# The background work of an eighteen-unit Strassen stage is placed step by step, and part of it changes engine

## The chip, the cores and the metric

The kernel runs on one core of one Trainium2 chip. The metric is the device time of one execution in microseconds (us). A program on this core issues instructions in a fixed order on each of five engines: TensorE (PE, matmuls; its weight loads are listed apart as PEld), VectorE (DVE), ScalarE (ACT), GpSimd (POOL) and SyncE (SP, which issues the DMAs). An engine that waits for something holds up all that stands behind it in its own order.

## The reference

```
attn = softmax-with-decay attention of q, k, v, f          (4 batches, 8 heads, 576 rows, 64 columns)
x    = attn, heads side by side                            (2304 x 512)
x    = (sigmoid(x @ w_gate) * (x @ w_val)) @ w_out         (w_gate, w_val: 512 x 1536, w_out: 1536 x 512)
logits = x @ router                                        (2304 x 8)
each token goes to one of 8 experts, at most 288 tokens each, in the order of the logits
out  = relu(x[mask_e] @ w1[e]) @ w2[e]                     (per expert, 512 -> 1024 -> 512)
```

## The kernel before

The program has five stretches: attention up to 195 us, the gated product with w_gate and w_val by a Strassen scheme (195 to 608 us), the product with w_out together with the router's dots (608 to 757 us), the routing, and the experts up to the end.

Because the order decides the experts, products are made in three passes: every operand is split into a high part (a copy by ACT into the matmul type) and a low part (the rest, a subtraction), and a product is high*high + high*low + low*high.

**The Strassen stage.** Class `Ffn`, method `unit` (L610). There are 18 units, listed in `UNITS`; a unit (p, t) makes columns p of gate and val for a third t of the tokens. It runs 14 products (`STEPS`: seven for gate, seven for val), each of six matmuls at L597. Units with t = 0 or 1 multiply 512 token columns at a time and are called wide here; those with t = 2 have 128 and are called narrow. Counted from 0 the narrow units are 3, 5, 8, 11, 14 and 15. Within a unit the base work is: ACT copies sums out of the accumulators (L620, L631) and takes the sigmoid (L641), DVE adds (L629), subtracts (L639) and multiplies gate by val (L647), SP stores (L605). PE waits for some of these: a product adds into an accumulator that an L629, L631 or L620 must have read or written.

**Background work.** While units run, operands of later ones are prepared. Class `Sets`: 48 pieces of weights come as 64-bit numbers and are packed to 32 bits by three DVE operations each (`bits`, L443, L445, L447). Pieces 0 to 23 go two by two into a set: tile `mb` holds the pair, four sums and differences of halves (`sums`, L465, L467, L468, L470, on DVE) make the Strassen operands, and ACT and GpSimd split them (`high` L484, `low` L488). There are 12 sets; a unit uses two. Pieces 24 to 47 are packed in the only buffer of tile `mw`, written back to memory by SP (`wf<-mw`, L450), and read again as w_out. Class `XOps` does the same for x: DVE multiplies the loaded attention result by the loaded 1/sum (`mult` L530, `mult_rest` L546), DVE adds (`add`, L551), and ACT and GpSimd or DVE split (L560, L564). Class `Out` splits w_out in 12 blocks (`weights`, L682, eight by GpSimd and four by DVE), and loads and splits the gated result (`load` L697, `split` L703, L704).

What sets their order: every unit gets one list of background operations, and after each product a like share of what is left of the list is issued:

```
n = -(-len(tasks) // (len(STEPS) - step))
for do in tasks[:n]:
    do()
tasks = tasks[n:]
```

The lists are filled in `network`: set 3 in unit 0, x of the second third in unit 1, x of the last third and the first pieces in unit 2, then a set or two with two pieces in each wide unit. The narrow units have no list. Pieces 32 to 37 stand in unit 13, 38 to 43 in unit 16, and 44 to 47 in unit 17, behind the splits of w_out; in unit 17 the first four splits of the gated result come last.

**After the stage.** `stream` (L722) makes one 128-token tile of x after another: 36 matmuls (L709), a copy by ACT into `mr`, a store, and eight dots on DVE with the router's columns (`dots`, L719). 12 of the 18 token tiles go this way, which makes 96 dots. The logits of the other six come from matmuls with a product of w_out and the router: `rest_logits` (L749 to L757) clears an accumulator on DVE at L753 and runs its matmuls, `logits` copies it (L765), transposes it on PE (L771) and copies it (L773). The matmuls at L757 therefore stand behind the DVE operations issued before L753.

Of the kernel before, what the change touches and what calls it, by code (L numbers as in the profile page):

```python
# [405 lines left out]
SEQ = list(range(12)) + sum(([12 + 2 * i, 13 + 2 * i, 24 + 2 * i, 25 + 2 * i] for i in range(4)), []) + list(range(20, 24)) + list(range(32, 48))  # L406
SLOT = {5: 0, 2: 1, 1: 2, 7: 3, 6: 4, 3: 5, 4: 6}
PART = {(0, 0): 2, (0, 1): 4, (1, 0): 3, (1, 1): 5}


class Sets:
# [19 lines left out]
    def bits(self, n, step, after=True):  # L431
        nc = self.ev.nc
        w = self.raw[n].bitcast(U32).rearrange("p (n t) -> p t n", t=2)
        if n < 2 * NF:
            if step == 0 and n % 2 == 0:
                self.b[n // 2] = self.mix.tile([128, 2, 512], U32, name="mb", bufs=1)
            b = self.b[n // 2][:, n % 2]
        else:
            if step == 0:
                self.b[n] = self.fw.tile([128, 512], U32, name="mw", bufs=1)  # L440
            b = self.b[n]
# [15 lines left out]
    def sums(self, s, step, tmp=None):  # L457
        nc = self.ev.nc
        b = self.halves(s)
        if step == 0:  # L460
# [4 lines left out]
            nc.vector.tensor_tensor(t, b[:, :, 0], b[:, :, 1], op=OP.add)  # L465
        elif step == 1:
            nc.vector.tensor_tensor(b[:, 1, 0], b[:, 1, 0], b[:, 0, 0], op=OP.subtract)  # L467
            nc.vector.tensor_tensor(b[:, 0, 1], b[:, 0, 1], b[:, 1, 1], op=OP.subtract)  # L468
        else:
            nc.vector.tensor_tensor(b[:, 0, 0], b[:, 0, 0], b[:, 1, 1], op=OP.add)  # L470
# [19 lines left out]
    def jobs(self, s):  # L490
        do = lambda f, *a: (lambda: f(*a))
        return [do(self.sums, s, 0), do(self.high, s, 2), do(self.sums, s, 1), do(self.low, s, 2), do(self.high, s, 0),
                do(self.low, s, 0), do(self.sums, s, 2), do(self.high, s, 1), do(self.low, s, 1)]

    def piece(self, n, after=True):
        do = lambda k: (lambda: self.bits(n, k, after))
        return [do(k) for k in range(3)]


class XOps:  # L500
# [1135 lines left out]
```

## Time and profile before

| what | us |
|---|---|
| runs shown: median (lowest, highest) of 3 | 1064.77 (1062.83, 1065.18) |
| the profiled execution | 1065.7 |
| its span, first to last instruction | 1063.5 |
| PE busy in the span | 953.4 (90%) |
| DVE, ACT, POOL busy | 597.8, 432.3, 475.6 |
| mean granted clock of TensorE, of full speed | 0.905 |

The span is what the trace shows, from the first instruction to the last; the profiled execution's time is 2.2 us longer. Stretches are given in us from the span's start. A row of the views below with an arrow names what an engine waited for and what ended the wait.

### The profile page before, as it was taken

The page shows a single profiled execution, that of the slowest core. Times are in us where ns is not written, and L with a number is a line of the kernel's source. Part 1 is how long each engine was busy: PE and PEld are TensorE (multiplying, and loading weights), DVE is VectorE, ACT ScalarE, POOL GpSimd, SP SyncE. Part 2 cuts the span into 40 slices and gives each one's busy share as a digit, 9 for nine tenths or more (in the row PEclk, how much of TensorE's full clock was granted, in tenths as well). Part 3 has the DMA queues.
Part 4 walks back from the last instruction along what each step waited for, and adds up shares of the span by engine and source line. Part 5 has one row for each costly group of instructions (what it writes and reads, how often), then busy time and mean ns, then how long its engine had stood idle before and what let it go on. Part 6 is the DMA issues. An engine that isn't in the chain of part 4 may idle for free. (4 is left out here: it accounts for less than half of the span.)

```text
span 1063.5 us, 15366 instructions
## 1 busy us (share of the span) xinstructions
PE 953.4 (90%) x5440; PEld 818.6 (77%) x5440; DVE 597.8 (56%) x1220; ACT 432.3 (41%) x798; POOL 475.6 (45%) x379
## 2 busy tenths in 40 slices
PE   8999999975799979897898679996599999999996
PEld 5787777753688778686796458885478999999996
DVE  6476755985544655657425649999554244333441
ACT  6777766642332333324212423222011554554431
POOL 7779886531111111112000438744022887777751
PEclk9999999997876978969659889899699999999998
DMA  4978786432322542534505767563112776666620
GB/s 125 256 213 209 206 229 166 132 91 72 109 59 59 149 131 71 151 112 139 161 18 168 267 238 278 178 229 116 48 41 81 224 225 205 199 198 182 197 91 29
DMA packets 92965, 160.87 MB, mean 151 GB/s; under 512 B 14995, under 2 KB 43059, under 8 KB 92758
## 3 DMA queue, kind: packets, MB, share of 16 engines
q1 hardware_dynamic: 88726, 148.34, 46.2%
q0 software_dynamic: 3072, 9.44, 2.7%
q10 hardware_dynamic: 1088, 2.10, 0.7%
q8 instruction: 43, 0.70, 0.3%
q14 instruction: 36, 0.29, 0.1%
HBM read 115.44 MB, written 35.01 MB: 141 GB/s over the span
## 5 line engine op out<-in xcount | busy, mean ns | idle before, releaser
L1095 POOL TENSOR_TENSOR elo<-eraw,ehi 128x1024 fp32r<-128x1024 f32 x46 | 110.9, 2421 | 34.8 <-ACT ehi L1093 34.5
L719 DVE CUSTOM_DVE_ANT_0 mb<-mr,bc 128x512 f32<-128x512 f32 x96 | 115.5, 1203 | 15.7 <-ACT mr L733 11.4
L160 PE MATMUL pv<-e,vf 128*65 128x256 f32 (+1 forms) x434 | 96.7, 360 | 0.0
L1189 PE MATMUL ey<-hh,ehi 128*128 128x288 f32 x256 | 77.8, 304 | 0.0
L1189 PE MATMUL ey<-hl,ehi 128*128 128x288 f32 x256 | 75.8, 296 | 0.5
L1189 PE MATMUL ey<-hh,elo 128*128 128x288 f32 x256 | 75.3, 294 | 0.0
L182 DVE CUSTOM_DVE_ANT_0 mj<-p1b,mq 128x192 bf16<-128x192 f32 (+1 forms) x116 | 42.3, 421 | 55.5 <-PE p1b L160 55.5
L160 PEld LDWEIGHTS pv<-e,vf 128*65 128x65 f32 x434 | 51.3, 139 | 21.2 <-issue 5.7
L1174 PE MATMUL eh<-xeh,ehi 128*128 128x288 f32 x224 | 67.6, 302 | 0.0
L1093 ACT ACTIVATE ehi<-eraw 128x1024 fp32r<-128x1024 f32 x60 | 63.4, 1056 | 9.3 <-DMA eraw<-w 9.3
L1174 PE MATMUL eh<-xeh,elo 128*128 128x288 f32 x224 | 65.9, 294 | 0.0
L1174 PE MATMUL eh<-xel,ehi 128*128 128x288 f32 x224 | 65.8, 294 | 0.0
L1177 DVE SCALAR_TENSOR_TENSOR hl<-eh,hh 128x288 fp32r<-128x288 f32 x64 | 29.1, 457 | 62.2 <-ACT hh L1176 52.0
L160 PE MATMUL p1b<-P 67*128 67x448 f32 (+2 forms) x244 | 58.6, 306 | 0.0
L682 POOL TENSOR_TENSOR wol<-wol,woh 128x512 fp32r<-128x512 f32 x8 | 12.0, 1526 | 98.7 <-ACT woh L682 98.7
L157 POOL TENSOR_TENSOR p<-raw,p 64x576 fp32r<-64x576 f32 x32 | 47.9, 1497 | 6.3 <-DMA p<-P 3.4
L647 DVE TENSOR_TENSOR q<-q,u 128x512 f32<-128x512 f32 (+1 forms) x36 | 25.8, 717 | 43.5 <-ACT u L620 43.5
L1176 ACT ACTIVATE hh<-eh 128x288 fp32r<-128x288 f32 x64 | 26.2, 411 | 57.2 <-PE eh L1174 41.8
L1189 PEld LDWEIGHTS ey<-hl,ehi 128*128 128x128 f32 x256 | 48.2, 188 | 1.6 <-DVE hl L1177 1.6
L704 POOL TENSOR_TENSOR a0l<-a0l,a0h 128x768 fp32r<-128x768 f32 x14 | 28.7, 2053 | 44.0 <-ACT a0h L703 41.9
L153 POOL TENSOR_TENSOR p<-raw,P 64x576 fp32r<-64x576 f32 x32 | 46.5, 1454 | 3.5 <-DMA p<-P 0.9
L1189 PEld LDWEIGHTS ey<-hh,ehi 128*128 128x128 f32 x256 | 48.1, 188 | 0.0
(603 smaller groups left out, 3013.3 us busy)
## 6 DMA issues: line engine op xcount, KB each, us to landing
eraw<-w SPq DMA_DIRECT2D x56, 512.0 KB
mr<-ww SPq DMA_DIRECT2D x36, 512.0 KB
gd<-q SPq DMA_DIRECT2D x96, 128.0 KB
p<-P SPq DMA_DIRECT2D x62, 144.0 KB
raw<-qk SPq DMA_DIRECT2D x15, 576.0 KB
wf<-mw SPq DMA_DIRECT2D x24, 256.0 KB
mr<-wt SPq DMA_DIRECT2D x12, 512.0 KB
a0l<-gd SPq DMA_DIRECT2D x14, 384.0 KB
```

Source lines behind the costliest of these rows:

```text
L153: nc.gpsimd.tensor_tensor(P2[h][64:128, :S], RAW[h][0:64], P1[h % 5][0:64, Q0:K0], op=OP.subtract)
L157: nc.gpsimd.tensor_tensor(p2[0:64, S:], r[64:128], p2[64:128, S:], op=OP.subtract)
L160: nc.tensor.matmul(out, lhsT, rhs, start=start, stop=stop, skip_group_check=True)
L182: nc.vector.tensor_tensor_reduce(out=junk[:, JT[t]:JT[t] + n], in0=src, in1=ev.mq[:, S - n:], op0=OP.add, op1=OP.min, scale=-1.0, scalar=3 ...
L704: (eng or nc.gpsimd).tensor_tensor(l, l.bitcast(F32), h, op=OP.subtract)
L719: nc.vector.tensor_tensor_reduce(out=junk, in0=x, in1=self.bc[:, e], op0=OP.mult, op1=OP.add, scale=1.0, scalar=0.0, accum_out=self.L[:, e ...
L1093: nc.scalar.activation(hi, r, AF.Copy)
L1095: eng.tensor_tensor(lo, r, hi, op=OP.subtract)
L1174: nc.tensor.matmul(p[:, :CH], w_[:, ws], x_[:, k], start=n == 0, stop=n == 11)
L1176: nc.scalar.activation(h[0][:, f], p[:, :CH], AF.Relu)
L1177: nc.vector.scalar_tensor_tensor(h[1][:, f], p[:, :CH], 0.0, h[0][:, f], op0=OP.max, op1=OP.subtract)
L1189: nc.tensor.matmul(p[:, :CH], w_[:, ws], h_[:, f], start=n == 0, stop=n == 23)
```

## The change

What it does:

1. Each background operation of the stage gets a step of its own, counted from 0 to 251 over the 18 units of 14 products, by `on(step, operation)`; `piece`, `wset` and `conv` place a piece, a weight set and an x operand. `unit` issues what stands at a step after its product. Narrow units have one piece each now, its three operations some four steps apart.
2. The four sums of weight halves go to GpSimd for sets 3 to 11. All low parts of x in the stage go to GpSimd (nine of them were on DVE), and so do all 12 splits of w_out.
3. Set 3 moves from unit 0 to steps 10 to 16. The x work of the second third is spread over units 0 to 2; x for the last third and its 1/sum are loaded ahead of the multiplications, in three groups, and multiplied in two operations instead of four.
4. The pieces above 30 use three buffers in turn (`mw` and the halves of `mb`). They stand two or three steps apart: 31 to 35 in units 12 and 13, one in each of units 14 and 15, 38 to 42 in unit 16, and 43 to 47 in unit 17, the last at step 247.
5. w_out is loaded at steps 224 to 235 (unit 16) and split at 227 to 238; the first four parts of the gated result are loaded at 238 and 239 and split at 242 to 246.
6. The accumulator of the router logits is cleared after 80 of the 96 dots instead of after all (`cleared`), in another bank.
7. In the attention, some loads of x are issued ahead of those of 1/sum.

The diff, cut to its core:

```
     def sums(self, s, step, tmp=None, eng=None):
+        eng = eng or self.ev.nc.gpsimd
...
-            nc.vector.tensor_tensor(t, b[:, :, 0], b[:, :, 1], op=OP.add)
+            eng.tensor_tensor(t, b[:, :, 0], b[:, :, 1], op=OP.add)
...
+                i = (n + 2) % 3 if n > 30 else 0
+                if i == 1:
+                    self.spare = self.mix.tile([128, 2, 512], U32, name="mb", bufs=1)
+                self.b[n] = self.spare[:, i - 1] if i else self.fw.tile([128, 512], U32, name="mw", bufs=1)
...
-    def mult_rest(self, k):
-        r = self.r4[:, k]
-        self.ev.nc.vector.tensor_tensor(r, self.x4[:, k], r, op=OP.mult)
+    def mult_rest(self, n):
+        x = self.x4[:, 2 * n:2 * n + 2]
+        self.ev.nc.vector.tensor_tensor(x, x, self.r4[n], op=OP.mult)
...
-    def unit(self, p, t, tasks):
+    def unit(self, n, plan):
...
-            n = -(-len(tasks) // (len(STEPS) - step))
-            for do in tasks[:n]:
+            for do in plan.pop(0, ()):
                 do()
-            tasks = tasks[n:]
+            for g in sorted(plan):
+                plan[g - 1] = plan.pop(g)
...
-        return [do(nc.scalar.activation, h, l.bitcast(F32), AF.Copy),
-                do((nc.vector if f % 3 == 2 else nc.gpsimd).tensor_tensor, l, l.bitcast(F32), h, op=OP.subtract)]
+        nc.scalar.activation(h, l.bitcast(F32), AF.Copy)
+        nc.gpsimd.tensor_tensor(l, l.bitcast(F32), h, op=OP.subtract)
...
+    def cleared(self):
+        self.lg = self.bank("o2")
+        self.ev.nc.vector.memset(self.lg[:, :256], 0.0)
...
     def rest_logits(self, raws):
-        self.lg = self.bank("o0")
-        nc.vector.memset(self.lg[:, :256], 0.0)
...
+        def on(g, f, *a, **k):
+            todo.setdefault(g, []).append(do(f, *a, **k))
...
+        def piece(n, *at):
+            for i, g in enumerate(at if len(at) == 3 else (at[0], at[0], at[-1])):
+                on(g, W.bits, n, i)
+
+        def wset(s, *at):
+            for n, g in enumerate(at if len(at) == 6 else [at[0] + i for i in (0, 1, 2, 3, 5, 6)]):
+                on(g, W.step, s, n)
...
+        wset(3, 10, 11, 12, 13, 15, 16)
...
+        on(24, lambda: X.load_x4(tmp["mr1"]))
+        on(22, lambda: X.load_r4(0, tmp["mb"][:, 512:]))
...
+        piece(8, 45, 49, 53)
+        piece(9, 56, 57)
+        wset(4, 58)
+        piece(24, 61, 62)
...
+        wset(11, 178)
+        for n, g in enumerate(((182, 183), (185, 186), (187, 188), (189, 190), (191, 192), (198, 202, 206), (212, 216, 220),
+                     (224, 225), (226, 227), (228, 229), (230, 231), (232, 233), (238, 239), (240, 241), (242, 243), (244, 245), (246, 247))):
+            piece(31 + n, *g)
...
+        for n in range(NF):
+            on(224 + n, O.load_weights, n)
+            on(227 + n, O.weights, n)
...
+        for n in range(4):
+            on(238 + n // 2, first, *divmod(n, 2))
+            on(242 + n + n // 2, O.split, line[n // 2], n % 2)
...
+        after[10][1].append(O.cleared)
```

How the order on the engines moves, at three places (`L` numbers are those of each program's own text; 128x512 is partitions by elements; `mr` is a piece as loaded, `q` and `u` are tiles of the unit's base work).

DVE in unit 13, the pieces; before:

```order
L447 SCALAR_TENSOR_TENSOR mw<-mr_4395,mw 128x512
L443 TENSOR_SCALAR mw<-mr_4410 128x512
L647 TENSOR_TENSOR q_4418<-q_4418,u_4449 128x512
L445 SCALAR_TENSOR_TENSOR mw<-mr_4410,mw 128x512
L447 SCALAR_TENSOR_TENSOR mw<-mr_4410,mw 128x512
L443 TENSOR_SCALAR mw<-mr_4432 128x512
L639 TENSOR_TENSOR q_4484<-gW,u_4474 128x512
L445 SCALAR_TENSOR_TENSOR mw<-mr_4432,mw 128x512
L647 TENSOR_TENSOR q_4461<-q_4461,u_4496 128x512
L447 SCALAR_TENSOR_TENSOR mw<-mr_4432,mw 128x512
L639 TENSOR_TENSOR q_4511<-gX,u_4487 128x512
L443 TENSOR_SCALAR mw<-mr_4465 128x512
```

and now:

```order
L445 TENSOR_SCALAR mb<-mr_4309 128x512
L447 SCALAR_TENSOR_TENSOR mb<-mr_4309,mb 128x512
L645 TENSOR_TENSOR vW<-u_4393,vD 128x512
L449 SCALAR_TENSOR_TENSOR mb<-mr_4309,mb 128x512
L445 TENSOR_SCALAR mb<-mr_4385 128x512
L447 SCALAR_TENSOR_TENSOR mb<-mr_4385,mb 128x512
L667 TENSOR_TENSOR q_4402<-q_4402,u_4433 128x512
L449 SCALAR_TENSOR_TENSOR mb<-mr_4385,mb 128x512
L445 TENSOR_SCALAR mw<-mr_4416 128x512
L447 SCALAR_TENSOR_TENSOR mw<-mr_4416,mw 128x512
L449 SCALAR_TENSOR_TENSOR mw<-mr_4416,mw 128x512
L659 TENSOR_TENSOR q_4472<-gW,u_4460 128x512
```

Before, the next piece's first operation (L443) writes the one buffer `mw` that the last piece's store still reads; now three pieces in a row have three different buffers (two of them halves of `mb`).

GpSimd in the middle of the stage, two weight sets before:

```order
L488 TENSOR_TENSOR a0l<-mb,a0h 128x512
L488 TENSOR_TENSOR a0l<-mw,a0h 128x512
L488 TENSOR_TENSOR a0l<-mb,a0h 128x768
L488 TENSOR_TENSOR a1l<-mb,a1h 128x512
L488 TENSOR_TENSOR a1l<-mw,a1h 128x512
L488 TENSOR_TENSOR a1l<-mb,a1h 128x768
```

and one set now:

```order
L467 TENSOR_TENSOR mw<-mb 128x512
L490 TENSOR_TENSOR a0l<-mb,a0h 128x512
L490 TENSOR_TENSOR a0l<-mw,a0h 128x512
L469 TENSOR_TENSOR mb<-mb 128x256
L470 TENSOR_TENSOR mb<-mb 128x256
L472 TENSOR_TENSOR mb<-mb 128x256
L490 TENSOR_TENSOR a0l<-mb,a0h 128x768
```

The four sums (L467, L469, L470 and L472) stand between the low parts (L490) now, where they were on DVE before.

DVE at the end of the router's dots; before:

```order
L719 ISA mb_6035,L_94<-mr1_6020,bc_5179 128x512
L719 ISA L_94 128x1
L719 ISA mb_6037,L_94<-mr1_6020,bc_5179 128x512
L719 ISA L_94 128x1
L753 MEMSET o0_6039 128x256
L1575 MEMSET mr0_6125 128x512
```

and now:

```order
L738 ISA mb_5899,L_94<-mr1_5884,bc_5167 128x512
L738 ISA L_94 128x1
L738 ISA mb_5901,L_94<-mr1_5884,bc_5167 128x512
L738 ISA L_94 128x1
L770 MEMSET o2_5946 128x256
L738 ISA mb_5951,L_94<-mr0_5948,bc_5167 128x512
L738 ISA L_94 128x1
```

The clearing of the accumulator (128x256) came behind the last dot; now it comes between the dots of the tenth tile and those of the eleventh.

## Rows read from the trace of the kernel before

**Rows 1.** Busy time by stretch. Columns: stretch, length, busy us by engine, granted clock, DMA share, GB/s.

```profile
195.50:215.00 19.50, 19.35 (x85) 15.69 (x84) 17.58 (x22) 11.57 (x20) 8.75 (x6) 1.00 0.66 187
215.00:241.00 26.00, 19.98 (x83) 14.85 (x82) 21.17 (x28) 10.72 (x20) 9.78 (x7) 1.00 0.28 83
215.00:280.10 65.10, 46.12 (x169) 34.33 (x168) 40.13 (x61) 25.56 (x50) 17.85 (x15) 0.90 0.24 66
280.10:302.50 22.40, 16.76 (x86) 16.28 (x84) 8.35 (x19) 4.35 (x15) 0.00 (x0) 0.62 0.46 135
302.50:323.20 20.70, 20.70 (x85) 17.00 (x85) 11.32 (x20) 9.08 (x16) 6.71 (x5) 0.92 0.26 70
323.20:326.40 3.20, 1.88 (x17) 1.71 (x15) 3.17 (x6) 1.58 (x3) 0.44 (x1) 0.99 0.30 82
361.30:403.70 42.40, 36.39 (x169) 31.85 (x168) 22.89 (x41) 12.77 (x31) 4.57 (x3) 0.81 0.47 141
403.70:467.70 64.00, 59.03 (x254) 50.31 (x254) 34.74 (x62) 21.36 (x45) 8.98 (x6) 0.82 0.40 119
467.70:515.90 48.20, 42.72 (x170) 34.03 (x170) 33.87 (x52) 17.22 (x30) 9.46 (x6) 0.91 0.46 139
515.90:535.50 19.60, 16.72 (x86) 16.23 (x84) 7.57 (x17) 4.35 (x15) 0.00 (x0) 0.63 0.42 128
535.50:553.40 17.90, 17.90 (x85) 17.90 (x85) 2.94 (x10) 3.32 (x13) 0.00 (x0) 0.50 0.05 15
553.40:608.30 54.90, 44.50 (x169) 34.18 (x169) 29.29 (x41) 18.79 (x35) 11.96 (x8) 0.89 0.60 203
608.30:636.40 28.10, 17.56 (x68) 14.01 (x68) 12.31 (x15) 6.20 (x10) 8.61 (x5) 0.82 0.65 222
```

**Rows 2.** Waits of PE, 195 to 612 us: what it waited for, total us, times, longest.

```profile
PE gB L597 <- ACT u L620: 16.8, 9, 4.3
PE vB L597 <- ACT u L620: 14.8, 9, 5.8
PE vW L597 <- DVE vW L629: 14.1, 6, 4.4
```

**Rows 3.** Groups by line and shape, 195 to 610 us: busy us, mean ns, idle before.

```profile
L465 DVE TENSOR_TENSOR mw<-mb 128x512 f32<-128x512 f32 x10 | 8.0, 799 | 0.3
L564 POOL TENSOR_TENSOR x1l<-mr,x1h 128x512 fp32r<-128x512 f32 x7 | 8.9, 1278 | 21.0 <-ACT x1h L560 21.0
L682 POOL TENSOR_TENSOR wol<-wol,woh 128x512 fp32r<-128x512 f32 x8 | 12.0, 1526 | 98.7 <-ACT woh L682 98.7
```

**Rows 4.** Timeline around the end of unit 4 and the start of unit 5.

```profile
318.15 0.43 DVE L467 TENSOR_TENSOR mb<-mb 128x256 f32<-128x256 f32 x1
318.30 1.42 POOL L488 TENSOR_TENSOR a1l<-mb,a1h 128x512 fp32r<-128x512 f32 x1 [5.23 <-ACT a1h L484]
318.49 1.51 DVE L468 TENSOR_TENSOR mb<-mb 128x256 f32<-128x256 f32 x1
322.80 1.39 DVE L647 TENSOR_TENSOR q<-q,u 128x512 f32<-128x512 f32 x1 [2.19 <-ACT u L620]
325.99 0.33 PE L597 MATMUL vB<-x2h,a3h 128*128 128x128 f32 x1 [1.32 <-ACT u L620]
```

**Rows 5.** Waits of DVE, 195 to 612 us.

```profile
DVE mw L443 <- DMA wf<-mw: 26.7, 12, 2.3
DVE mr L546 <- DMA mr<-rec: 12.7, 4, 6.8
```

**Rows 6.** Timeline: the first router dot, and the end of the router logits.

```profile
636.42 1.85 DVE L719 CUSTOM_DVE_ANT_0 mb<-mr,bc 128x512 f32<-128x512 f32 x1 [11.39 <-ACT mr L733]
...
765.86 0.38 ACT L765 ACTIVATE mr<-o 96x256 f32<-96x256 f32 x1 [20.82 <-PE o L757]
768.59 0.21 DVE L773 COPY L<-gv 128x48 f32<-128x48 f32 x1 [10.26 <-PE gv L771]
```

**Rows 7.** The page's costliest groups: the router dots.

```profile
L719 DVE CUSTOM_DVE_ANT_0 mb<-mr,bc 128x512 f32<-128x512 f32 x96 | 115.5, 1203 | 15.7 <-ACT mr L733 11.4
```

More of the change, by code (lines that the diff above doesn't have):

```diff
@@ L488, in low, with step @@
         self.ev.nc.gpsimd.tensor_tensor(lo, x, hi, op=OP.subtract)
[L490 to L497, printed above, removed]
+    def step(self, s, n):
+        if n == 0:
+            self.sums(s, 0)
+        if n == 1 or n == 2 or n == 5:
+            self.low(s, (None, 2, 0, None, None, 1)[n])
+        if n == 2 or n == 3:
+            self.sums(s, n - 1)
+        if n == 0 or n == 1 or n == 4:
+            self.high(s, (2, 0, None, None, 1)[n])
 class XOps:
@@ L608, in store @@
             self.ev.nc.sync.dma_start(self.gd[4][j, :, f], s)
-    def unit(self, p, t, tasks):
+    def unit(self, n, plan):
         nc = self.ev.nc
+        p, t = UNITS[n]
         T = TC if t < 2 else 128
-        s = {}
-        held = []
-        tasks = list(tasks)
+        s, held, at = {}, [], 0
+        if t == 2 and UNITS[n - 1][1] == 2:
+            at = 128
+        elif t == 2:
+            self.short = [self.fw.tile([128, 512], F32, name=f"q{i}", bufs=1) for i in range(3)]
         def copied(x):
@@ L1439, in bounced @@
-        def bounced(a, b):
-            return sum((W.piece(n) for n in range(a, b)), [])
-        def pair(p, s, after=True):
-            n = 4 * p + 2 * s
-            return [W.piece(n, after), W.piece(n + 1, after), W.jobs(2 * p + s)]
-        T = {u: [] for u in UNITS}
-        a, b, c = pair(1, 1, False)
-        d = W.jobs(2)
-        T[0, 0] = d[:5] + W.last[1:] + [do(xload, 1, 0, rs[4]), do(xload, 1, 2, rs[5])] + d[5:] + a + b + c
-        order = ((4, None), (3, V), (1, None), (2, V), (7, None), (5, V), (6, None))
@@ new lines, in conv @@
+        def conv(t, i, m, ga, gh, gl, s=None):
+            b = blocks[i if t == 1 else 2]
+            c = i if t == 1 else slice(0, 2)
+            if m in (2, 5):
+                x = lambda: b[11 if m == 2 else 22]
+            elif m == 6:
+                x = lambda: b[12]
+            else:
+                x = (lambda: s()) if t == 1 else (lambda: s().rearrange("p (k s) -> p k s", k=2))
+            if ga is not None:
+                on(ga, lambda: X.add(x(), m, b))
+            on(gh, lambda: X.high(t, m, c, x()))
+            on(gl, lambda: X.low(t, m, c, x()))
@@ new lines, in network @@
+        W.last[0]()
+        for k, r in ((0, 0), (2, 1), (1, 2), (3, 3)):
+            xload(0, k, rs[r])
+        V = nc.vector
+        on(0, W.sums, 2, 0, eng=V)
+        on(0, W.high, 2, 2)
+        on(1, W.low, 2, 2)
+        on(1, W.sums, 2, 1, eng=V)
+        on(1, W.high, 2, 0)
+        on(2, W.low, 2, 0)
+        on(2, W.sums, 2, 2, eng=V)
+        on(3, W.high, 2, 1)
+        on(4, W.low, 2, 1)
+        xmult(5, 0, 0)
+        on(4, W.last[1])
+        on(5, W.last[2])
+        xmult(10, 0, 2)
@@ L1455, in rest @@
+        conv(1, 0, 5, None, 28, 29)
+        conv(1, 1, 5, None, 30, 31)
+        conv(1, 0, 7, 30, 31, 32, block("mw"))
+        conv(1, 0, 6, 31, 32, 33)
+        on(31, X.mult_rest, 0)
+        on(32, lambda: X.load_r4(1, tmp["mb"][:, 512:]))
+        conv(1, 1, 7, 32, 33, 34, block("mb"))
+        conv(1, 1, 6, 33, 34, 35)
+        on(36, W.load, 8)
         def rest():
[L1456 removed]
             X.tiles(2, x4)
[L1458 removed]
@@ L1477, in network, with unit @@
+        def unit(n):
+            now = {g - 14 * n: todo.pop(g) for g in sorted(todo) if g < 14 * n + 14}
+            F.unit(n, now)
         F.mark()
-        for u in UNITS[:-2]:
-            F.unit(*u, T[u])
+        for n in range(16):
+            unit(n)
         later.close()
```

201 lines of the change are left out of this document (116 added, 85 removed).

## The prediction

> **What bounds the kernel now.** I read the busy time by stretch first, then the waits of PE and DVE, and last the timeline at the places those name. In the Strassen stage no engine is full. The yardstick is a unit in which PE never waits: 19.5 us for a wide unit that follows a wide one, 20.7 for one that follows a narrow one (it begins at the lower clock), and 17.9 for a narrow one at half clock [rows 1] (the stretches from 195.50, 302.50 and 535.50). The 18 units last 412.8 us, 195.5 to 608.3; where they exceed the yardstick, PE is idle: in units 1 and 2 it is busy 46.12 of 65.10 us, with DVE at 40.13. PE waits there for copies by ACT and additions by DVE [rows 2], which are short themselves and queue behind background work. Behind the stage the limit changes: from 636.42 [rows 6] DVE does 96 dots of 1.203 us [rows 7], and the matmuls of the last logits can't start before them.
>
> **The clock.** [...] Idleness alone did not lower it: between 215 and 241 us PE was busy 19.98 of 26.00 and the clock stayed at 1.00 [rows 1]. Narrow work entered with a wait did: unit 5 ran at .99 until 326.4, PE waited 1.32 us at 325.99 [rows 4], and the clock fell. Unit 15 began at half clock and stayed there although PE was busy 17.90 of 17.90. So a narrow unit that enters at full clock without such a wait may keep it, and one that has lost it won't regain it. What the wait hung on: ACT's copy stood behind a DVE multiplication that took 1.39 us [rows 4], beside 0.80 for a sum of the same size [rows 3].
>
> **The change part by part**, against the profiled 1065.7 us:
>
> *Units 1 and 2*, 65.1 us. The x operands are spread over units 0 to 2, the late x loads no longer hold up DVE (12.7 us in four waits [rows 5]), nine low parts leave DVE. It had 17.58 + 40.13 = 57.7 us of work in units 0 to 2; off come set 3's sums (0.80 and three of 0.43 [rows 3, 4], 2.1) and nine low parts (six of about 0.8, three of 0.43: 6.1), leaving 49.5 in some 62. GpSimd takes over some 10 (six of 1.278 [rows 3], three of half that) and slows DVE beside it. I take two wide units plus 3.5 for such waits: 42.5, a gain of 22.6; ends 39.0 and, if all ten of GpSimd's are added, 52.5.
>
> *Unit 3* (narrow, 22.4): its x work remains; 17.9 + 1.0, gain 3.5. *Units 4 to 6*: nothing, they are near the yardstick already. *Units 7 and 8*, 42.4: 19.5 + 17.9 + 1.1 = 38.5, gain 3.9. *Units 9 to 11*, 64.0: 20.7 + 19.5 + 17.9 + 0.5 = 58.6, gain 5.4. *Units 12 and 13*, 48.2: the sums leave DVE and the pieces no longer wait for the store of the one before (26.7 us in 12 waits over the stage [rows 5]), so 20.7 + 19.5 = 40.2, gain 8.0. *Units 14 and 15*, 37.5: 35.8 + 0.6, gain 1.1. For each the ends are no gain and the yardstick.
>
> *Units 16 and 17*, 54.9. GpSimd gets 12 splits of 1.5 us [rows 3], 18 us; DVE loses four of them and gets pieces 38 to 47, ten of about 1.8 us (three operations of some 0.5 to 0.8, by the sums of rows 3), besides base work. The loads come to some 8 MB in unit 16 (12 of 256 KB for w_out, five pieces of 512 read and 256 written, the gated stores), some 350 GB/s where the stretch now moves 203 [rows 1]; ACT's copies wait in order for w_out. I take 48, between 40.2 and 54.9: gain 6.9.
>
> *Last product to first dot*, 28.1 us. The pieces and splits that PE and ACT waited for end within unit 17 now. What is left is 36 matmuls of 0.258 us (17.56 by 68 [rows 1]), 9.3, a copy and the hand-overs: 11.5, gain 16.6. If the first splits are late: 20, gain 8. The 96 dots stay as they are.
>
> *Router logits.* The clearing comes 16 dots earlier, so PE's matmuls run under the dots. Behind the last dot remain the copy, the transposes and the copy at 768.59, 2.7 us after 765.86 [rows 6]; of DVE's 10.26 us of waiting 8.6 go, 0 if PE is late. *Attention*: x loaded ahead takes one short wait or two off; 1.0, ends 0 and 2. *Two more loads* of 512 KB in the stage, and the narrow units' own pieces on DVE (three of 0.8 in 18 us): nothing, since DVE is busy 8.35 of 22.40 there at most [rows 1]; without that cover about 1 us a unit.
>
> Sum: 22.6 + 3.5 + 3.9 + 5.4 + 8.0 + 1.1 + 6.9 + 16.6 + 8.6 + 1.0 = 77.6, which gives 988.
>
> *The narrow units' clock.* 17 narrow matmuls at full clock kept PE busy 1.88 us [rows 1] (the stretch from 323.20), 0.11 each, so 84 take 9.3 where they take 17.9, and the next unit is spared the slow start, 1.2: 9.8 each. Units 5, 11, 14 and 15 have little background work in the five steps ahead of them, 3 and 8 have x work or a set's last low part. Of these four I take two: 19.6 less, 969 against the profiled execution. That stood 0.9 above the median of the runs, so **968**.
>
> [...] A GpSimd low part ran from 318.30 for 1.42 us, and the 256-column difference that DVE began at 318.49 took 1.51 where the one before took 0.43 [rows 4]: it ended when GpSimd's did. [...] So a sum moved to GpSimd is not off DVE: four sums of a set cost DVE 0.80 + 3 x 0.43 = 2.1 us there, and on GpSimd some 1.28 + 3 x 0.64 = 3.2 us in which DVE may stand still. If it stood still for all of them, nine sets would add 9 x 1.1 = 10 us to DVE instead of relieving it by 19, most of it under PE.
>
> **The rivals.**
> - *No narrow unit keeps the clock* (18%): every one lost it before. 988 less 0.9, 987. For it: the clock is at half at the end of all of them. Against it: unit 5, whose entry rows 4 show, had a wait that goes.
> - *All four keep it* (12%): 2 x 9.8 less, 948. [...]
> - *GpSimd and DVE in each other's way* (15%): units 1 and 2 at 52.5 (10 lost), 16 and 17 no better (7), the way to the first dot 20 (8), 10 on the other sets, no clock kept: 987 + 35 = 1022, in all from 1000 to 1050.
> [...]
> - *Nothing moves* (3%): the waits of rows 2 go to other waits of the same length, 1065. The order shows that the operations do move, so I give it little.
>
> **How the numbers follow.** The forecast, one to three narrow units at full clock and the stages near the sums above, has 46%. The range reaches from a little below the second rival, with the better ends of units 1, 2, 16 and 17 counted in part, to the lower part of the third: **938 to 1012** leaves out some 2 in 10. A change under 0.2%, 2 us, couldn't be told from none. Faster takes the forecast and the first three rivals, 91%; within 0.2% 3%; slower 6%.
>
> **What would show it.** Right: units 1 and 2 last 39 to 46 us; DVE's wait for `wf<-mw` falls from 26.7 to under 5; first dot within 13 us of the last product; the matmuls of the last logits run before the last dot ends; the clock is 1.00 in one to three narrow units. Wrong: DVE operations of 256 columns with a mean over 1 us beside GpSimd and PE waits at L597 as long as before; GpSimd operations over 2.5 us; ACT idle for `wol<-wf` over 5 us in units 16 and 17; a first dot later than 20 us behind the last product.

## The result, and the profile after

The changed kernel takes 968.73 us (median of 4 runs, 963.92 to 974.66), the kernel before 1064.97 (4 runs, 1062.83 to 1069.27): a ratio of 0.9094, 95% interval 0.9033 to 0.9156. The forecast was 968, in a range of 938 to 1012. One run of all those below, 991.65 us with the clearing behind the last dot, is over 1.5% slower than the fastest of its kernel; it counts as slow and is left out of the times given.

The busy time by stretch of the changed kernel, in the columns of [rows 1]; the stretches are units 0, 1 and 2, 3, 4, 5, 6, 7 and 8, 9 to 11, 12 and 13, 14, 15, 16 and 17, and the way from the last product to the first dot:

```profile
191.40:210.70 19.30, 19.27 (x85) 15.65 (x84) 17.82 (x22) 11.78 (x20) 10.64 (x8) 1.00 0.56 169
210.70:255.40 44.70, 39.57 (x169) 31.16 (x169) 37.54 (x42) 23.32 (x45) 31.00 (x23) 1.00 0.51 139
255.40:272.30 16.90, 15.01 (x86) 14.69 (x84) 9.07 (x20) 5.66 (x19) 3.62 (x5) 0.68 0.35 92
272.30:292.70 20.40, 20.40 (x85) 16.77 (x85) 10.72 (x17) 8.43 (x15) 8.34 (x7) 0.93 0.39 119
292.70:302.10 9.40, 9.40 (x86) 9.36 (x85) 6.83 (x14) 4.05 (x14) 1.48 (x2) 1.00 0.49 129
302.10:321.20 19.10, 19.10 (x86) 15.80 (x85) 12.37 (x21) 9.16 (x18) 12.20 (x11) 1.00 0.47 144
321.20:359.50 38.30, 35.95 (x170) 32.50 (x168) 22.32 (x37) 14.00 (x32) 11.68 (x10) 0.79 0.45 128
359.50:409.50 50.00, 49.77 (x254) 42.52 (x254) 28.60 (x51) 21.43 (x45) 16.94 (x15) 0.96 0.43 127
409.50:447.60 38.10, 38.10 (x170) 31.55 (x169) 24.13 (x40) 17.23 (x31) 15.86 (x14) 1.00 0.59 173
447.60:465.10 17.50, 15.52 (x86) 15.38 (x84) 8.61 (x19) 4.32 (x15) 0.00 (x0) 0.64 0.48 145
465.10:483.00 17.90, 17.90 (x86) 17.90 (x85) 4.46 (x13) 3.32 (x13) 0.00 (x0) 0.50 0.19 57
483.00:529.00 46.00, 40.92 (x169) 32.41 (x168) 36.70 (x42) 21.44 (x37) 26.21 (x16) 0.96 0.84 280
529.00:547.60 18.60, 15.18 (x56) 12.29 (x56) 6.24 (x12) 4.05 (x7) 0.45 (x1) 0.82 0.72 261
```

Beside the forecast (its sum for each part, with no narrow unit at full clock; then 19.6 less for two of them), in us of the profiled executions, whose time after was 970.97:

| part | before | forecast | after |
|---|---|---|---|
| attention, up to unit 0 | 195.5 | 194.5 | 191.4 |
| unit 0 | 19.5 | 19.5 | 19.3 |
| units 1 and 2 | 65.1 | 42.5 | 44.7 |
| unit 3 | 22.4 | 18.9 | 16.9 |
| units 4 to 6 | 58.8 | 58.8 | 48.9 |
| units 7 and 8 | 42.4 | 38.5 | 38.3 |
| units 9 to 11 | 64.0 | 58.6 | 50.0 |
| units 12 and 13 | 48.2 | 40.2 | 38.1 |
| units 14 and 15 | 37.5 | 36.4 | 35.4 |
| units 16 and 17 | 54.9 | 48.0 | 46.0 |
| last product to first dot | 28.1 | 11.5 | 18.6 |
| 96 dots | 120.7 | 120.7 | 120.3 |
| last dot to the copy of the logits | 11.5 | 2.9 | 3.4 |
| routing and experts | 294.9 | 294.9 | 298.0 |
| two narrow units at full clock | | -19.6 | (in units 4 to 6 and 9 to 11) |

Two of the four narrow units did keep the clock: unit 5 stands by itself, 9.40 us at 1.00, and unit 11 is why units 9 to 11 take 50.0:

```profile
399.70:409.50 9.80, 9.57 (x86) 9.43 (x84) 6.50 (x16) 4.09 (x15) 0.50 (x1) 1.00 0.44 132
```

Units 14 and 15 fell: 0.64 and 0.50. So did units 3 and 8, of which I had not expected more. Wide units from 4 to 13 now take 19.0 to 19.2 us, or 20.5 and 21.2 behind a narrow unit that ended at a clock of 0.50 (units 4 and 9), and PE waits in none of them.

The waits of PE in the stage; then one that [rows 2] leaves out, of the kernel before; then the wait of DVE that answers to the first of [rows 5]:

```profile
PE vB L610 <- ACT u L636: 10.6, 7, 2.4
PE gB L610 <- ACT u L636: 3.7, 3, 1.7
PE gW L610 <- POOL x1l L577: 2.2, 2, 2.0
```

```profile
PE gW L597 <- DVE gW L629: 9.4, 9, 5.0
```

```profile
DVE mw L445 <- DMA mr<-ww: 2.2, 1, 2.2
```

The three waits of [rows 2] were 45.7 us together, and with the one for DVE's additions into `gW` 55.1; the three above are 16.5, and the additions at L629 (L645 now) are no longer among them. DVE's 26.7 us of waiting for `wf<-mw` are gone from the list; in their place the pieces' first operations wait for loads and for GpSimd's low parts, 2.2 us at the longest. The way to the first dot, in the timeline of the changed kernel:

```profile
532.47 0.79 PE L728 MATMUL o<-woh,a0h 128*128 128x512 f32 x1 [3.42 <-ACT u L636]
...
546.23 0.85 ACT L722 ACTIVATE a0h<-a0l 128x768 fp32r<-128x768 f32 x1 [11.34 <-DMA a0l<-gd]
...
547.59 1.95 DVE L738 CUSTOM_DVE_ANT_0 mb<-mr,bc 128x512 f32<-128x512 f32 x1 [11.19 <-ACT mr L752]
```

PE starts this product 3.4 us late, behind ACT's last copy. The 36 matmuls, the first 12 of them at a granted clock of 0.50, are through at 543.3; but ACT's copy of their tile stands behind the split of a later tile (546.23), which waited 11.34 us for its load, so it runs at 546.98 and the first dot is at 547.59. And the end of the logits:

```profile
654.39 0.27 DVE L770 MEMSET o<- 128x256 f32 x1
...
654.71 0.38 PE L778 MATMUL o<-q,wp 128*8 128x128 f32 x1 [5.75 <-DVE o L770]
...
668.09 0.38 ACT L786 ACTIVATE mr<-o 96x256 f32<-96x256 f32 x1 [12.26 <-DVE L L738]
...
668.52 2.73 PE L792 MATMUL gv<-ident,mr 96*128 96x8 f32 x12 [5.50 <-ACT mr L786]
...
671.29 0.21 DVE L794 COPY L<-gv 128x48 f32<-128x48 f32 x1 [2.53 <-PE gv L792]
```

The accumulator is cleared at 654.39, with 16 dots to come, the matmuls run under them, and the copy at 671.29 comes 3.4 us after the last dot, where it came 11.5 us after it [rows 6]. PE, idle for 5.50 us before the transposes, takes 2.73 us for them, and the first 11.4 us of the routing run at a clock of 0.86, where they ran at 1.00.

### The profile page after: what moved, and what is told of

Read it like the earlier page. It is cut to its first block, busy times and chain, and to the rows that moved or that the text cites. A ratio compares the mean times of both kernels' runs of the same rounds, so it can differ in the third digit from the quotient of the medians.

```text
span 969.3 us, 15340 instructions
## 1 busy us (share of the span) xinstructions
PE 917.7 (95%) x5440; PEld 794.6 (82%) x5440; DVE 583.4 (60%) x1169; ACT 432.0 (45%) x798; POOL 532.3 (55%) x428
## 5 line engine op out<-in xcount | busy, mean ns | idle before, releaser
L1116 POOL TENSOR_TENSOR elo<-eraw,ehi 128x1024 fp32r<-128x1024 f32 x46 | 110.8, 2418 | 36.4 <-ACT ehi L1114 35.7
L467 POOL TENSOR_TENSOR mw<-mb 128x512 f32<-128x512 f32 x9 | 12.0, 1334 | 96.4 <-DVE mb L449 78.1
L160 PE MATMUL p1b<-P 67*128 67x448 f32 (+2 forms) x244 | 58.6, 307 | 0.0
L667 DVE TENSOR_TENSOR q<-q,u 128x512 f32<-128x512 f32 (+1 forms) x36 | 30.6, 850 | 38.5 <-ACT u L636 36.6
L704 POOL TENSOR_TENSOR wol<-wol,woh 128x512 fp32r<-128x512 f32 x12 | 17.4, 1468 | 62.9 <-ACT woh L703 62.8
L1210 PEld LDWEIGHTS ey<-hl,ehi 128*128 128x128 f32 x256 | 48.2, 188 | 2.7 <-DVE hl L1198 2.7
```

Of the source, the lines that this page charges most:

```text
L160: nc.tensor.matmul(out, lhsT, rhs, start=start, stop=stop, skip_group_check=True)
L667: nc.vector.tensor_tensor(s[q], s[q], x, op=OP.mult)
L1116: eng.tensor_tensor(lo, r, hi, op=OP.subtract)
L1210: nc.tensor.matmul(p[:, :CH], w_[:, ws], h_[:, f], start=n == 0, stop=n == 23)
```

## The experiments

Each kernel was run beside the kernel before on the same chip, four executions of each unless said otherwise, and seven or more of the kernel before. Runs of one kernel differ by 5 to 14 us here, so what a median can't tell is read from the profile, unit by unit.

### Clearing the entries of units 8 and 14

In the changed kernel's timeline at the entry of unit 14, which starts at 447.6:

```profile
443.16 0.43 DVE L445 TENSOR_SCALAR mw<-mr 128x512 uint32<-128x512 uint32 x1 [2.16 <-DMA mr<-ww]
...
448.54 0.68 DVE L449 SCALAR_TENSOR_TENSOR mb<-mr,mb 128x512 uint32<-128x512 uint32 x1
...
449.14 0.68 DVE L659 TENSOR_TENSOR q<-gX,u 128x512 f32<-128x512 f32 x1
...
449.86 0.63 ACT L661 ACTIVATE q<-q 128x512 f32<-128x512 f32 x1 [2.58 <-DVE q L659]
...
451.03 0.33 PE L610 MATMUL vB<-x2h,a1h 128*128 128x128 f32 x1 [1.98 <-ACT u L636]
```

Piece 34 waits 2.16 us for its load on DVE, and piece 35 starts after another 1.22 us in which DVE is idle and the profile names no cause; so pieces 34 and 35, at steps 189 to 192, come late, and the subtraction at 449.14 behind them, the sigmoid, ACT's copy (at 450.40), and PE behind that: 1.98 us. (Pieces 31 to 35 all stand in unit 13, steps 182 to 192, and not in units 12 and 13 as the description of the change has it.) The edit:

```
-        piece(26, 98, 99)         ->  piece(26, 97, 98)
-        piece(14, 100, 101)       ->  piece(14, 99, 100)
-        piece(15, 102, 103)       ->  piece(15, 101, 102)
-        wset(7, 104)              ->  wset(7, 103)
-        piece(27, 107, 108)       ->  piece(27, 112, 113, 115)
-        piece(16, 116, 119, 122)  ->  piece(16, 117, 120, 123)
- pieces 34 to 37: (189, 190), (191, 192), (198, 202, 206), (212, 216, 220)
+                  (197, 199, 201), (204, 206, 208), (211, 213, 215), (218, 220, 222)
```

> The changed kernel with one edit: background work is taken out of the last steps ahead of narrow units 8 and 14. Piece 35 goes from steps 191 and 192 into unit 14, pieces 34 to 37 are spread over units 14 and 15, piece 27 goes from steps 107 and 108 into unit 8, and set 7 with pieces 26, 14 and 15 comes one step earlier. Theory (a narrow unit falls to half clock because of the wait of 1.5 to 2.4 us at its entry, and that wait is DVE work issued just ahead): the waits fall under 0.7 us, units 14 and 15 run in 9 to 10 us each and unit 8 perhaps, 18.4 to 28 us less: 940 to 952 us. Rival (narrow work falls to half clock in any case and units 5 and 11 were luck): units 14 and 15 stay at 17 to 18 us and the time within 4 of 968.7.

Measured: 947.38 us (942.53 to 948.12), ratio 0.8892 (0.8836 to 0.8948). Units 8, 14 and 15, by stretch:

```profile
346.10:355.40 9.30, 9.30 (x85) 9.27 (x84) 7.36 (x17) 4.10 (x15) 1.49 (x1) 1.00 0.65 185
441.50:450.90 9.40, 9.40 (x86) 9.37 (x84) 6.15 (x16) 3.08 (x13) 0.00 (x0) 1.00 0.56 155
450.90:460.20 9.30, 9.30 (x86) 9.30 (x85) 5.72 (x17) 3.11 (x14) 0.00 (x0) 1.00 0.64 198
```

All three run at full clock, with more pieces in units 14 and 15 than before. No work was taken away: the same instructions stand some steps earlier or later, and 21 us are gone. The mean granted clock of the four runs, 0.966 to 0.976 against 0.942 to 0.950 in the four of the changed kernel, says the same of the executions that have no profile. That units 5 and 11 had been luck is excluded. Whether an earlier load of piece 34 alone would have done for unit 14 was not tried.

### The reverse, in unit 5

A first try moved pieces 24 and 10 to steps 65 and 66 of the changed kernel (`piece(24, 61, 62)` to `piece(24, 65)`, `piece(10, 66, 67)` to `piece(10, 66)`).

> The changed kernel with one edit, the reverse of the last: pieces 24 and 10 are moved to steps 65 and 66, so that six DVE operations stand ahead of the subtraction whose sigmoid and copy the first products of narrow unit 5 wait for. The same work, some 5 us later. Theory: PE waits 1.5 us or more at the entry of unit 5, the clock falls, and unit 5 takes 17 to 18 us instead of 9.3 and unit 6 begins slowly: 8 to 10 us slower, 976 to 980. Rival (the wait alone costs, the clock is not tied to it): 1 to 3 us slower, unit 5 at full clock.

Measured: 965.81 us (965.10 to 977.70), and unit 5 at full clock in 9.6 us. It told neither theory from the other, since no wait arose: the subtraction came 0.4 us ahead of the unit's start, and PE found the copy ready. The second try was made on the last kernel, with both pieces at step 66 (`piece(24, 66)`, `piece(10, 66)`).

> The kernel with the entries of units 8 and 14 cleared, with one edit: pieces 24 and 10 are both packed at step 66, six DVE operations (3.6 us) in a row ahead of the subtraction that unit 5's entry waits for. At steps 65 and 66, in an earlier run, the subtraction came 0.4 us ahead of the unit's start and no wait arose; in the changed kernel's unit 14, which fell, it came 1.5 us behind. Here it should come about 1.4 us behind. Theory (the wait takes the clock): PE waits 1.3 to 2 us at the entry, unit 5 runs at half clock, 17 to 18 us, and unit 6 starts slowly: 8 to 10 us slower, 955 to 958. Rival (a wait costs itself only): 1 to 2 us slower, 948 to 950, clock 1.00 in unit 5.

Measured: 948.88 us (945.13 to 951.51). The entry of unit 5, which starts at 285.2, and unit 5 by stretch:

```profile
286.55 0.68 DVE L659 TENSOR_TENSOR q<-gX,u 128x512 f32<-128x512 f32 x1
...
287.81 0.58 ACT L636 ACTIVATE u<-vB 128x512 f32<-128x512 f32 x1
...
288.44 0.33 PE L610 MATMUL vB<-x2h,a3h 128*128 128x128 f32 x1 [1.80 <-ACT u L636]
```

```profile
285.20:302.80 17.60, 15.80 (x86) 15.65 (x84) 8.86 (x18) 5.37 (x17) 3.67 (x3) 0.63 0.48 142
```

The subtraction is 1.35 us behind the unit's start, PE waits 1.80 us, and the unit takes 17.60 us at 0.63 instead of 9.3 at 1.00; unit 6 begins slowly, 21.0 instead of 19.2. So a wait of 1.80 us costs some 10. The medians don't show it: 1.5 us, where 8 to 10 were expected. In the profiled execution other differences hide it: unit 3 kept its clock, which it hadn't in the profile of the kernel compared with (units 2 to 4 take 7.8 us less), and the attention ended 4.8 us sooner. Why the other three runs moved as little is not known; the effect is shown by the profile alone.

### Unit 3

This was not tried by an edit; it is what the profiles of the twelve changed versions show (all but the one made from the kernel before). Unit 3 kept its clock in six and fell in six. Units 2 and 3 in one that kept it, the version with the clearing behind the last dot:

```profile
235.90:261.70 25.80, 21.90 (x86) 16.67 (x85) 21.22 (x25) 14.39 (x30) 19.86 (x14) 0.93 0.39 103
261.70:271.10 9.40, 9.40 (x85) 9.32 (x84) 6.41 (x15) 4.86 (x18) 2.94 (x4) 1.00 0.45 126
```

and unit 2 of the changed kernel, whose unit 3 fell (0.68, in the first table), with the longest wait of PE in that unit 3:

```profile
231.30:255.40 24.10, 20.17 (x85) 15.43 (x84) 19.55 (x21) 13.68 (x28) 18.90 (x14) 1.00 0.38 99
```

```profile
258.48 0.33 PE L610 MATMUL vB<-x2h,a1h 128*128 128x128 f32 x1 [1.56 <-ACT u L636]
```

In all six that kept it, the clock had dipped within unit 2 (0.93 here) and was back at full for unit 3; of the six others, unit 2 stayed at 1.00 in five, and unit 3 lost it. At the end of unit 2 the wait is the same, PE for a low part on GpSimd, 1.94 to 1.96 us in the ten versions that make it there. At the start of unit 3 it is not: where the clock had dipped, PE came to unit 3 1.7 us later, and ACT's copy was there (in the version above it ended at 262.43, and the product that needs it began at 262.94 without a wait). PE idled at most 0.34 us in unit 3 in the six that kept the clock; of the six that lost it, one had as little (the attention's loads as before, below, whose unit 2 had dipped too) and five 0.96 to 1.90. A dip in the wide unit costs 1.7 us (25.80 for 24.10), in the narrow one 7.5 (16.90 for 9.40). That this is most of the 10 us by which runs of the changed kernel differ is likely, but there is only one profile of each kernel.

The narrow units of all 14 profiles, the kernel before and its version with three buffers included, go the same way. 75 of the 84 entered at full clock. 43 of these kept it, and PE idled at most 0.37 us in each; 32 lost it, one with 0.34 us of idle PE (the unit 3 named above) and 31 with 0.54 to 5.75. The shortest of these, 0.54 us, was in unit 11 of the version that clears the accumulator 8 dots from the end: 15.5 us at 0.63. The other nine are unit 15 behind a unit 14 that had lost the clock, and all nine ran at 0.50 throughout.

### The sums of weight halves back on DVE

```
-        eng = eng or self.ev.nc.gpsimd
+        eng = eng or self.ev.nc.vector
```

> The changed kernel with one edit: the four sums of weight halves of sets 3 to 11 go back to VectorE, at the same steps. Theory (the sums matter because DVE's queue delays the additions that PE waits for): nine sets put 9 x 2.1 = 19 us back on DVE, most of it beside idle DVE; the stretch of units 0 to 2 gains 2 to 4 us, and a narrow unit may lose its clock (9.8 each) where a sum falls in the unit before: 972 to 985 us. Rival (the placement by steps is the whole gain, the engine is indifferent): within 3 us of the changed kernel's 968.7, and the same units at full clock. [...]

Measured: 974.87 us (968.08 to 981.85). The time lies in the theory's range, but the medians differ by 6 and the ranges overlap; the profiled execution had unit 3 at full clock, and apart from units 2 to 4 its stage is 2 us longer than the changed kernel's. The same edit on the kernel with cleared entries:

> The kernel with the entries of units 8 and 14 cleared (median 947.4), with one edit: the sums of sets 3 to 11 go back to VectorE at the same steps. In the changed kernel the same edit gave 974.9 against 968.7, with which units kept the clock differing from run to run; here the narrow units but one keep it, so that less is left to that. Theory (DVE's queue is what PE waits for): 4 to 12 us slower, by gaps of PE in wide units, or by a narrow unit that falls. Rival (GpSimd and VectorE stand in each other's way as much as they help): within 3 us of 947.4, with PE's waits in the stage within 2 us.

Measured: 948.33 us (943.30 to 951.86), against 947.38: the rival's time. PE's waits are the theory's: 3.9 us more in the stage, where the rival had them within 2. By unit, PE idles 0.5 to 1 us more in units 1, 7, 13 and 17; the stage takes 312.6 us against 308.9, though unit 3 is 1 us shorter. So the engine of the sums is worth 2 to 4 us of the stage in the profiles, which the medians can't tell from none: a small part of the gain.

### Three buffers alone, in the kernel before

```
-                self.b[n] = self.fw.tile([128, 512], U32, name="mw", bufs=1)
+                i = (n + 2) % 3 if n > 30 else 0
+                if i == 1:
+                    self.spare = self.mix.tile([128, 2, 512], U32, name="mb", bufs=1)
+                self.b[n] = self.spare[:, i - 1] if i else self.fw.tile([128, 512], U32, name="mw", bufs=1)
```

> The kernel before with one edit: pieces above 30 use three buffers in turn instead of one. Nothing else is changed. Theory (DVE's waits for the store of the piece before, 26.7 us, delay additions in units 13, 16 and 17 and the way to the first dot): 6 to 14 us faster than before, 1051 to 1059, with the waits under 8 us. Rival (the waits are given back to the next transfer, the load of the next piece): within 3 us of before.

Measured: 1045.49 us (1039.48 to 1047.42), against 1066.74 for the kernel before on the same chip; ratio 0.9803 (0.9731 to 0.9875). More than expected. DVE's wait for the store, and units 13, 16, 17 and the way to the first dot:

```profile
DVE mw L446 <- DMA wf<-mw: 4.4, 2, 2.2
```

```profile
490.00:513.50 23.50, 19.98 (x85) 15.49 (x84) 16.00 (x28) 8.64 (x15) 4.15 (x3) 1.00 0.62 195
548.70:569.40 20.70, 20.70 (x86) 16.99 (x86) 11.77 (x22) 6.27 (x11) 0.00 (x0) 0.92 0.51 172
569.40:596.10 26.70, 21.20 (x85) 16.48 (x83) 17.85 (x22) 12.16 (x23) 11.96 (x8) 0.94 0.82 280
596.10:618.70 22.60, 13.53 (x49) 10.65 (x50) 8.61 (x14) 6.45 (x11) 8.04 (x5) 0.77 0.83 276
```

The wait falls from 26.7 to 4.4 us. Of the gain, 4.6 us are in unit 13 (28.1 of the 48.2 of units 12 and 13 before), 2.3 in unit 14 (19.6 before), 7.5 in units 16 and 17 (54.9) and 5.5 on the way to the first dot (28.1): a fifth of what the whole change gains, from a part of its item 4.

### The clearing of the logits' accumulator

Behind the last dot again (`O.cleared()` ahead of `O.rest_logits`):

> The changed kernel with one edit: the accumulator of the last logits is cleared behind the 96th dot again. Theory: PE's matmuls of the last logits, 8 us, come back onto the path between the last dot and the copy of the logits (3.4 us in the changed kernel, 11.5 before): 8 us slower, 974 to 980 us, with part of it given back by a PE that goes into the routing at the full clock. Rival (the matmuls were hidden and the routing waits for something else): 968.7 within 2.

Measured: 974.79 us (974.41 to 981.28, three runs). The copy of the logits comes 10.3 us after the last dot, against 3.4; the routing and experts take 295.5 us against 298.0. So in the profiles the early clearing gains 6.9 us at the place and gives 2.5 back behind it. With 8 dots to come instead of 16 (`after[11][1]` for `after[10][1]`):

> The changed kernel with one edit: the accumulator of the last logits is cleared with 8 of the 96 dots still to come instead of 16. PE stood idle for 5.5 us between these matmuls and the transposes, and ran the first stretch of the routing at a clock of 0.86. Theory (that idle time cooled PE): the matmuls now end about when the dots do, the 12 transposes take 1.4 us instead of 2.73, and the stretch up to the first choice of the routing is 1 to 2.5 us shorter: 966 to 968. Rival: PE's 8 us no longer fit under 8 dots (about 10 us) and reach past them: 1 to 3 us slower.

Measured: 974.31 us (967.07 to 977.50): not faster, and unit 11 lost its clock in the profiled execution (behind a wait of 0.54 us), which is 6 us. At the place itself the profile has the transposes

```profile
674.87 1.40 PE L792 MATMUL gv<-ident,mr 96*128 96x8 f32 x12
```

in 1.40 us instead of 2.73; the copy comes 4.0 us after the last dot, 0.6 more, and what follows takes 296.3 us, 1.7 less. So it was the idle time that slowed PE, and it is worth 1 us, which the medians can't show. All profiles agree: in the eight where PE was idle for 4.2 to 5.5 us just ahead of the transposes, these took 2.3 to 2.7 us and the clock of the next 11.4 us was 0.74 to 0.86; in the six without such a gap, 1.40 us and 1.00.

### The copy of the first tile ahead of the later splits

In `stream`, for the first tile alone, the copy by ACT, the store and the dots are issued ahead of `after[1]`.

> The changed kernel with one edit: in the first tile of the product with w_out, ACT's copy of the tile, its store and its dots are issued ahead of the background work of that tile's second half (a split of a later tile, which waits for its load). Theory (the first dot, 18.5 us after the last product, is late because ACT waits 11.3 us for that load): the first dot comes 2.5 to 4 us earlier and all 96 dots with it: 965 to 966. Rival (the dots wait for the router's columns, which are loaded at 537): the first dot stays within 1 us.

Measured: 974.26 us (968.15 to 978.31). The first dot comes 16.1 us after the last product instead of 18.6; but the 96 dots take 122.6 us instead of 120.3. DVE's waits there:

```profile
DVE mb L738 <- DMA wg<-wgd: 8.6, 1, 8.6
DVE mb L738 <- ACT mr L752: 4.1, 1, 4.1
```

The tile's copy is done at 540.71, but DVE, idle for 8.6 us, starts the first dot at 542.52, behind the load of the router's columns, which is issued after the stage (it reads `bc`; the profile names `wg`, issued right behind it); and the second tile's copy is 4.1 us late in place of the first's. Both theories were half right, and the gain is given back by the next tile.

### The attention's loads as before

x and 1/sum are loaded together again, and multiplied at the steps of the kernel before.

> The changed kernel with one edit: in the attention, x and 1/sum are loaded together and multiplied at the steps of the kernel before. Theory: the Strassen stage begins at 195.5 instead of 191.4 us after the start, as in the kernel before: 3 to 5 us slower, 972 to 974. Rival, my forecast of that part: 1 us.

Measured: 973.10 us (966.34 to 975.61). The stage starts at 194.1. But in the other profiles, whose attention is the same throughout, it starts at 190.4 to 196.2. The 4.1 us between the two first profiles are within that; a gain of this part isn't shown.

### A version that beats both

The kernel with cleared entries, and three edits:

```
-        after[10][1].append(O.cleared)
+        after[11][1].append(O.cleared)
-            on(gl, lambda: X.low(t, m, c, x()))
+            on(gl, lambda: X.low(t, m, c, x(), V if t == 1 and m > 5 else None))
-            on(227 + n, O.weights, n)
+            on(230 + n, O.weights, n)
```

> The kernel with the entries of units 8 and 14 cleared, with three more edits: the logits' accumulator is cleared 8 dots from the end; the low parts of x1 for m = 7 and 6 (four operations) go to VectorE, since the longest wait of unit 2 was for one of them on GpSimd (1.95 us); the 12 splits of w_out are issued three steps later, since ACT waited 9.8 us for their loads and PE for ACT behind them. Theory: unit 2 loses 2 us and unit 3 keeps the clock more often (8 us), units 16 and 17 lose 3 to 5, the logits 1: 932 to 945. Rival (each wait is followed by another of the same length): 947 within 3.

Measured: 943.52 us (941.46 to 947.09), ratio 0.8876 (0.8818 to 0.8934), the fastest of the study, 25 us below the changed kernel. Against the 947.38 of the entries alone the gain is small and the ranges overlap, and the profiles don't bear it out: their stages take the same (310.0 us each), and the 4.4 us between the two executions are an attention that ended 4.3 us sooner. Unit 2 lost 0.8 us of the 2, unit 3 fell, and units 16 and 17 did not gain: ACT's wait for the loads of w_out went from 9.6 us to 0.2, but PE waited 5 us there as before, now for DVE in part, which is the rival's account. In unit 17 DVE's operations take longer beside GpSimd's (the first and the second of a piece 0.42 and 0.69 us alone):

```profile
490.62 4.26 POOL L723 TENSOR_TENSOR a0l<-a0l,a0h 128x768 fp32r<-128x768 f32 x2
...
491.73 1.45 DVE L445 TENSOR_SCALAR mb<-mr 128x512 uint32<-128x512 uint32 x1
...
493.21 2.22 DVE L447 SCALAR_TENSOR_TENSOR mb<-mr,mb 128x512 uint32<-128x512 uint32 x1
```

Operations of a piece beside GpSimd's splits of the gated result take 1.45 and 2.22 us here; beside those of w_out, earlier in the unit, 1.06 to 1.67. The last kernel moves the 12 splits of w_out to DVE (six executions):

> The last kernel (entries cleared, four low parts of x1 on VectorE, splits of w_out three steps later, logits cleared 8 dots from the end; median 943.5), with one edit: all 12 splits of w_out go from GpSimd to VectorE. In that kernel, pieces on VectorE that run beside a split on GpSimd take 1.1 to 2.2 us an operation, against 0.43 to 0.69 alone. Theory (the two engines exclude each other, so that 12 splits of 1.5 us on GpSimd cost VectorE up to 17 us where 12 of 0.7 on VectorE cost it 8): the operations of the pieces fall to 0.4 to 1.0 us in unit 17, units 16 and 17 lose 1 to 4 us of 44.8, and the way from the last product to the first dot (20.0 us) 0 to 3: 937 to 942. Rival (VectorE, already busy 80% of these units, becomes the bound): 2 to 6 us slower, 945 to 950.

Measured: 947.77 us (942.52 to 950.97). Groups of DVE in units 16 and 17, then PE's longest wait there:

```profile
L447 DVE SCALAR_TENSOR_TENSOR mb<-mr,mb 128x512 uint32<-128x512 uint32 x7 | 6.4, 908 | 0.2
...
L445 DVE TENSOR_SCALAR mb<-mr 128x512 uint32<-128x512 uint32 x7 | 3.0, 423 | 4.9 <-DMA mr<-wt 4.9
```

```profile
PE vW L610 <- DVE vW L645: 3.6, 1, 3.6
```

The first operation of a piece is at 0.42 us, as it is alone (0.81 in the kernel before this edit), the second at 0.91 (1.19); three operations beside the splits of the gated result, which stay on GpSimd, still take 2.2 to 2.3 us. The first dot comes 16.6 us after the last product instead of 20.0. But the splits stand in DVE's order ahead of the additions, PE waits 3.6 us for one, the clock falls (0.83 in unit 17), and units 16 and 17 take 51.4 us instead of 44.8. The theory's first half held for the most part and its sum didn't; the 4 us between the medians are within the spread of the runs.

## Why the prediction was right, and where it wasn't

**What bounds the stage** held. PE's idle time went with the placement, to the yardstick, in the wide units from 4 to 13; the forecast of each stretch of the stage without the clock is within 2.5 us of the profile. For its largest term, units 1 and 2 (20.4 us gained, 22.6 forecast), the profile has DVE's waits for the late x loads down from 12.7 us [rows 5] to 0.3; but no run gives the x work its old order or engine back, so how the 20.4 us divide among the parts of item 3 is not shown. Nor is the new layout of the narrow units' `q` tiles (`short` in the program), which the description of the change leaves out, taken apart.

**The clock** held, and became the strongest lever: narrow units that entered at full clock and without a wait kept it (43 of the 44 in which PE idled at most 0.37 us), two of four did, and both directions were then made to happen by moving work. With five narrow units at full clock the cleared entries took 947.38 us, near the 948 that the second rival had for four. Unit 15 fell because 14 had: PE was busy for 17.90 of 17.90 us at 0.50 and the clock did not rise. Wide work differs: unit 4, behind a narrow unit that ended at 0.50, had 0.93 over its length, and unit 5 begins at 1.00; the narrow work of unit 15 kept PE as busy and stayed at 0.50.

**Which units would keep it** was half wrong in its reason. I said that 5, 11, 14 and 15 have little background work in the five steps ahead of them. For unit 14 that was read from the steps, and even by those the three operations of piece 35 stand in the five (191 to 195); in the timeline pieces 34 and 35 ran some two steps late, behind a load. It is the time at which they run that counts.

**The way to the first dot** was the one term clearly off: 18.6 for 11.5 us. Its step "36 matmuls of 0.258 us, a copy and the hand-overs" left out ACT's order (a split that waits for a load stands ahead of the copy), PE's 3.4 us behind ACT's last copy, and a third of the matmuls at a clock of 0.50. It was still within the bound of 20, but the sign of being right, a first dot within 13 us, did not come.

**Units 16 and 17** came at 46.0 for 48, though one sign of being wrong was there: ACT was idle for `wol<-wf` for 9.8 us, where I had set 5. Taking that wait away, in the fastest version, gained nothing there. DVE did not get ten pieces either: seven of them stood in these units before, and three behind the stage.

**The sums** were given as a reason for units 12 and 13 ("the sums leave DVE and the pieces no longer wait for the store"). The second half holds for the greater part: three buffers alone gave 4.6 us in unit 13, and putting the sums back on DVE cost 1.3 to 1.4 there and 2 to 4 in the whole stage. The four sums of a set took 4.05 us on GpSimd, for the 3.2 I had given them. What I had against moving them was seen again in DVE operations of 1.45 to 2.22 us beside GpSimd, against 0.42 to 0.69 alone (in rows 4 the DVE operation ended 0.28 us after GpSimd's, not with it, as I wrote), and yet it cost nothing that could be measured at the sums; it may be because DVE had time to spare there, which was not tried apart. Taking the splits of w_out off GpSimd, in the last run, cost more by the order of DVE's queue (units 16 and 17 took 51.4 us for 44.8).

**The router logits**: 8.6 forecast, 8.1 gained at the place, and some 2.5 to 3 given back in the routing, by a PE that had stood idle for 5.50 us (a clock of 0.86 over the first 11.4 us, where it was 1.00); I had not counted that. **The attention**: 1.0 forecast, not shown. **The rivals**: none came. GpSimd's 512-column sums took 1.33 us, far from the 2.5 that I had set as a sign of being wrong, a bound that no run shows.

So the total was nearer than its parts, and that is luck: 7 us too much on the way to the first dot and 3 behind it were made up but for 3 by 3 in the attention and 4 in the stage, and four runs of the changed kernel lie 10.7 us apart.

## What to carry to other kernels

Where one engine runs thin matmuls between wide ones, look at the instant at which it enters them: waits of 0.5 to 3 us there cost 6 to 10 us here, and moving a few background operations by some steps took them away. Place background work by when it will run, with its loads counted, not by the step that it is written at. Two more buffers for a tile that is stored and refilled (21 us, in the kernel before) were worth more than the choice of engine for 36 operations (2 to 4).

## What the hardware showed that I had not expected

- The clock's fall in unit 2 or 3 goes by execution: with the same program up to there, the profiles show a dip in unit 2 that costs 1.7 us, or one in unit 3 that costs 7.5.
- DVE's one-input operation on a piece, 0.42 us alone, took 1.45 beside GpSimd; one with two inputs, 0.68 to 0.69 alone, took 2.22.
- After an idle stretch of 5.50 us PE took 2.73 us for twelve small transposes that took 1.40 when it had been kept busy.
- GpSimd's splits hold up the router's dots as well. In the changed kernel's 120.3 us of dots, DVE is busy for 116.05; the 32 dots of 96 that begin beside one of GpSimd's 32 splits take 2.21 us on average, the others 0.69, some 49 us in all. It was the same before the change (2.22 and 0.69), and no run moves these splits. PE is busy for 109.68 us there, so far less than 49 us could come of it.

```profile
601.57 0.69 DVE L738 CUSTOM_DVE_ANT_0 mb<-mr,bc 128x512 f32<-128x512 f32 x1
601.82 2.15 POOL L723 TENSOR_TENSOR a1l<-a1l,a1h 128x768 fp32r<-128x768 f32 x1 [3.15 <-ACT a1h L722]
602.31 2.21 DVE L738 CUSTOM_DVE_ANT_0 mb<-mr,bc 128x512 f32<-128x512 f32 x1
```
